# A sketched-attention and expert kernel on one core: GpSimd's last sends behind the branch, VectorE for the last scaling, the head in written order

## The chip, the cores and the metric

The kernel runs on 1 core of one Trainium2 chip. The metric is device microseconds (us) of one execution; the time given is the median of several runs. The engines are called PE (TensorE), DVE (VectorE), ACT (ScalarE), POOL (GpSimd) and SP (SyncE). Each engine has a sequencer that walks through its own instructions in order; the profile writes PEq, DVEq, ACTq, POOLq and SPq for it. A load or store that SP, ACT or POOL issues is carried out by the DMA engines.

## What is computed

An attention block with sketched features, whose output, laid out as 4352 rows of 128, goes through a top-1 mixture of 8 experts with an output gate:

```python
a, b = S1 @ x, S2 @ x                       # phi(x): outer product of two sketches, r = 8, so 64 features
kv = einsum('bhsf,bhsd->bhfd', phi(k), v)
z = sum over s of phi(k)
attn = (phi(q) @ kv) / (phi(q) . z + 1e-6)  # 4 batches, 4 heads, 1088 positions, head size 32
x = attn as 4352 x 128
e = argmax(x @ w_gate); gate = softmax(x @ w_gate)[e]; eom = sigmoid(x @ w_output_gate)
out = gate * eom[e] * (relu(x @ w1[e]) @ w2[e])        # 128 -> 1024 -> 128 in expert e
```

## The kernel before

**Head.** The program begins with small tables. SP loads the two sketch matrices S1 and S2 (line 275, into `bits`, 2 KB each) and after them the first groups of k, q and v (`load`, lines 287 to 293). They are 64-bit numbers; `split` (lines 406 to 427) turns them into two fp32 parts on DVE, `turn_rows` transposes the parts on PE (line 403) and line 436 spreads them over the four heads into `Sb`, the matrix that every sketch multiplies with. While it waits, PE multiplies zeros (`zeros`, line 260). POOL writes the tables that routing needs much later: `ones`, `eio`, `eps`, `ecap`, `carry` (lines 331 to 342) and those of `pool_constants` (line 355); ACT blanks the buffers `kz` and `xin` (line 451) and copies `carry` into the first table of running sums (`choose_carry`, line 688). This part stands outside `tc.manual_schedule()`, so that a scheduler may move its instructions on each engine.

**Body.** Up to line 1124 the order is that of a planner (`Plan`): every step has an engine, a length, a rank (with the table `NUDGE`) and the steps it waits for, and `plan.order()` writes them out, engine by engine in that order. It covers the sketches (`sketch`), products (`both`, `product`), sums over k and v (`sums`), attention (`attend`), the routing of the rows to experts, and the 32 tiles of 128 rows that each expert gets four of whatever the counts are (`NF` = 32). For a tile t: `fetch` (POOL, an indirect DMA of the rows into `xin`), `divide` and `turn_copy` (DVE), `turn` (PE), `up` (PE, 8 products of 128 by 128), `relu` (ACT or DVE in turn), `down` (PE, 8 products), `scale` (ACT, line 929: the gate, from PSUM into `ys`) and `give` (POOL, line 933: an indirect DMA that scatters the rows of `ys` into the output).

**Late tiles.** How many tiles more are needed is known only at run time: a count `nt` (at most 33) is loaded into a register of every engine, and `arm` (line 1089) writes a cascade of nested branches. Arm k runs when nt > k:

```python
with tc.If(now["nt"] > k, label=f"exit{k}") as more:
    expect(k + 1)
    ...                      # loads, up(t), relu(t), down(t - 1)
    scale(t - 1)
    give(t - 1)
    arm(k + 1)
with more.Else():
    down(t - 1); scale(t - 1); give(t - 1)
```

with t = 32 + k. The code of all taken arms follows in one piece, and the Else parts stand behind it, that of the deepest arm first. `expect` puts a hint for the next branch into the programs of PE, ACT and POOL (line 1087: one register instruction and one BRANCH_PREFETCH_HINT). In the runs shown nt is 5: tiles 32 to 36 are late ones, arms 0 to 4 are taken, and at exit5 every engine jumps to an Else part, which holds the end of tile 36.

Of the kernel before, what the change touches and what calls it, by code (L numbers as in the profile page):

```python
# [177 lines left out]
def kernel(  # L178
# [40 lines left out]
    def const(name, shape, dtype=F32):  # L219
        return sbuf.tile(list(shape), dtype, tag=name, name=name)  # L220
# [33 lines left out]

    ys = [const(f"ys{i}", [TS, DM]) for i in range(NY)]
# [13 lines left out]
    for i, x in enumerate((S1, S2)):  # L269
        own = slice(i * r, (i + 1) * r)  # L270
        if wide:
            x, dst, n = x.bitcast(I32), bits[own].rearrange("p d w -> p (d w)"), 2 * D
        else:
            dst, n = plain[own], D
        nc.sync.dma_start(dst, bass.AP(tensor=x.tensor, offset=x.offset, ap=[[n, r], [1, n]]))
# [49 lines left out]
    for h in range(H):  # L325
        nc.vector.memset(maskh[h * D:(h + 1) * D, h:h + 1], 1.0)
    mask0 = const("mask0", [128, 1])
# [4 lines left out]
    nc.gpsimd.memset(ones, 1.0)  # L332
    eio = const("eio", [128, E])
    for e in range(E):
        nc.gpsimd.memset(eio[:, e:e + 1], float(e))
    eps = const("eps", [128, 1])
    nc.gpsimd.memset(eps, EPS)
    ecap = const("ecap", [128, E])
    nc.gpsimd.tensor_scalar_mul(ecap, eio, float(CAP))
    carry = const("carry", [128, E])  # L340
    nc.gpsimd.memset(carry, 0.0)
    nc.gpsimd.tensor_copy(carry[0:1], ecap[0:1])
# [42 lines left out]
    before, efirst, exs = pool_constants()  # L385
# [13 lines left out]
    turned_rows = ps_t()  # L399
    Sb = const("Sb", [128, 2, H, 2 * r])  # L400

    def turn_rows(i):
        nc.tensor.transpose(turned_rows[:, 2 * r * i:2 * r * (i + 1)], rows[i].rearrange("p h d -> p (h d)"), ident[:2 * r, :2 * r])
        zeros(1)

    def split():
# [20 lines left out]
        turn_rows(1)  # L427
    if wide:
        split()
    else:  # L430
        nc.vector.tensor_copy(rows[0], plain.unsqueeze(1).to_broadcast((2 * r, H, D)))
        turn_rows(0)
        nc.vector.memset(rows[1], 0.0)
        turn_rows(1)
    for i in range(2):
        nc.vector.tensor_mul(Sb[:, i], bview(turned_rows[:, 2 * r * i:2 * r * (i + 1)], [[0, H], [1, 2 * r]]),
                             bview(maskh, [[1, H], [0, 2 * r]]))

    selr = const("selr", [2 * D, 2])
    nc.vector.memset(selr, 0.0)  # L440
    for i in range(2):
        nc.vector.memset(selr[D * i:D * (i + 1), i:i + 1], 1.0)
# [555 lines left out]
    for i, rs in enumerate(routes):  # L998
# [6 lines left out]
        add(f"CC{i}", "ACT", 210, k, prior, lambda i=i: choose_carry(i))  # L1005
# [79 lines left out]
    def expect(k):  # L1085
        if k < NL:
            tc.mark_branch_hint_location(f"exit{k}", hint=now["nt"] > k, engines=[mybir.EngineType.PE, mybir.EngineType.Activation, mybir.EngineType.Pool])

    def arm(k):
        t = NF + k  # L1090
        if k == NL:
            down(t - 1)
            scale(t - 1)
            give(t - 1)
            return
        rings = (ps_t, ps_w, ps_y)
        kept = [(list(x.free), dict(x.lent)) for x in rings]
        with tc.If(now["nt"] > k, label=f"exit{k}") as more:
            expect(k + 1)
            if AHEAD <= k + 2 < NL:  # L1100
                fetch_weights(t + 2)
            if LA <= k + 3 < NL:
                fetch(t + 3)
            up(t)
            if LT <= k + 1 < NL:
                divide(t + 1)
                turn(t + 1)
                turn_copy(t + 1)
            relu(t, t % 2 == 0)
            down(t - 1)  # L1110
            scale(t - 1)
            give(t - 1)
            arm(k + 1)
        for x, (free, lent) in zip(rings, kept):
            x.free, x.lent = free, lent
        with more.Else():
            down(t - 1)
            scale(t - 1)
            give(t - 1)

    with tc.manual_schedule():
        for name in plan.order():
            plan.ops[name]["emit"]()
        arm(0)
# [36 lines left out]
```

## Time and profile before

| what | value |
|---|---|
| time, median of 3 runs | 208.14 us (207.84 to 208.62) |
| the profiled execution's own time | 208.37 us |
| its span | 206.6 us |
| PE busy | 193.3 us, 94% of the span |
| DVE, ACT, POOL busy | 105.1, 73.0, 87.4 us |
| loads and stores | 32.02 MB |

The span reaches from the first to the last instruction that the profiler recorded; the time has 1.8 us more around it. Busy time is given by engine; the time of a sequencer's own instructions (waits, branches, semaphores, issuing of DMAs) is not in it. In a timeline row the first number is the start in us from the span's start, the second the duration, and the bracket says how long the engine stood idle before it and what ended that. A row such as "MATMUL y<-xall,hT" names the tile written and the tiles read.

### The profile page before, as it was taken

The numbers are of one execution on the slowest core, as the hardware profiler recorded it, in microseconds if no ns is written. First come the engines' busy times: TensorE is split into PE (matmuls) and PEld (weight loads), VectorE is DVE, ScalarE is ACT, GpSimd is POOL, SyncE is SP. The second block draws the span as 40 slices with busy tenths as digits, with TensorE's granted clock in tenths as the row PEclk, the third lists the DMA queues.
The fourth block names the chain that finished last, engine by engine and source line by source line (L and its number), as shares of the span: only waits on it lengthen the run. The fifth ranks groups of instructions, "written<-read, shape, count | busy, mean of one in ns | idle before, by whom it ended". The sixth has DMA issues, their size and how long they took to land.

```text
span 206.6 us, 6180 instructions
## 1 busy us (share of the span) xinstructions
PE 193.3 (94%) x2530; PEld 185.8 (90%) x2530; DVE 105.1 (51%) x287; ACT 73.0 (35%) x173; POOL 87.4 (42%) x116
## 2 busy tenths in 40 slices
PE   7799999997999999999999989999999999999960
PEld 6699898876799999899999989999999999999960
DVE  5777878898774554775497144204312434311300
ACT  7226575476764244341132121231223022123120
POOL 8100000003826423767365727365347635354631
PEclk9789999999999999999999999999999999999996
DMA  4998878671259991271149992111101101016010
GB/s 143 337 360 241 285 263 286 206 230 41 64 141 344 312 376 32 70 246 57 37 123 405 412 416 83 52 32 48 40 20 50 49 12 53 18 33 219 16 38 13
DMA packets 14934, 32.02 MB, mean 155 GB/s; under 512 B 2489, under 2 KB 7751, under 8 KB 14000
## 3 DMA queue, kind: packets, MB, share of 16 engines
q1 hardware_dynamic: 9488, 17.49, 24.9%
q10 hardware_dynamic: 2304, 8.39, 11.5%
q0 software_dynamic: 3104, 5.65, 9.1%
q8 instruction: 22, 0.36, 0.7%
q14 instruction: 16, 0.13, 0.2%
HBM read 26.47 MB, written 5.84 MB: 156 GB/s over the span
## 4 chain that ended last, share of the span: by engine, by line
PE 51%; issue 17%; DMA 9%; POOL 8%; DVE 7%; ACT 4%; POOLq 1%; SPq 1%
PE w L913 15%; PE acc L926 8%; PE y L926 8%; PE w L496 5%; DMA xin<-xt,putf 5%; PE acc L559 4%; POOL out_dram L933 4%; POOL xin L889 4%; PE w L636 3%; PE w L609 3%; DMA kT<-in_k_dram 2%; DMA out_dram<-ys,putfar 2%; ACT xall L649 2%; ACT qpT L615 1%; PE t L903 1%
## 5 line engine op out<-in xcount | busy, mean ns | idle before, releaser
L889 POOL DMA_INDIRECT xin<-xt,putf x32 | 35.1, 1096 | 80.9 <-DVE ab L525 43.6
L913 PE MATMUL w<-xsT,wt 128*128 128x128 f32 x512 | 61.3, 275 | 0.0
L913 PEld LDWEIGHTS w<-xsT,wt 128*128 128x128 f32 x512 | 59.3, 192 | 0.2
L933 POOL DMA_INDIRECT out_dram<-ys,putf x32 | 34.0, 1064 | 16.1 <-ACT ys L929 8.2
L917 ACT ACTIVATE hT<-w 128x1024 f32<-128x1024 f32 x23 | 23.5, 1024 | 40.7 <-PE w L913 40.7
L926 PE MATMUL acc<-wt,hT 128*128 128x128 f32 x256 | 31.3, 275 | 0.7 <-DVE hT L919 0.7
L926 PE MATMUL y<-wt,hT 128*128 128x128 f32 x256 | 31.4, 276 | 0.0
L926 PEld LDWEIGHTS acc<-wt,hT 128*128 128x128 f32 x256 | 29.9, 192 | 0.9 <-issue 0.9
L919 DVE TENSOR_SCALAR hT<-w 128x1024 f32<-128x1024 f32 x14 | 17.1, 1223 | 25.9 <-PE w L913 24.4
L926 PEld LDWEIGHTS y<-wt,hT 128*128 128x128 f32 x256 | 30.0, 192 | 0.0
L906 DVE COPY xsT<-t 128x128 f32<-128x128 f32 x38 | 10.3, 286 | 24.8 <-PE t L903 24.8
L929 ACT ACTIVATE ys<-y,xin 128x128 f32<-128x128 f32 x19 | 7.0, 367 | 39.7 <-PE y L926 34.8
L899 DVE TENSOR_TENSOR xdiv<-xin 128x128 f32<-128x128 f32 x38 | 10.6, 286 | 20.2 <-DMA xin<-xt,putf 12.4
L929 ACT ACTIVATE ys<-acc,xin 128x128 f32<-128x128 f32 x18 | 6.6, 367 | 19.7 <-PE acc L926 19.0
L889 POOL DMA_INDIRECT xin<-xt,putfar x8 | 8.4, 1047 | 9.9 <-ACT ys L929 7.7
L559 PE MATMUL acc<-vt,kp 128*64 128x65 f32 (+1 forms) x288 | 11.7, 229 | 0.0
L559 PEld LDWEIGHTS acc<-vt,kp 128*64 128x64 f32 (+1 forms) x288 | 9.9, 140 | 1.9 <-issue 0.4
L636 PEld LDWEIGHTS w<-kz,qpT 64*64 64x64 f32 x544 | 8.7, 134 | 2.7 <-ACT qpT L615 1.8
L536 DVE TENSOR_TENSOR kp<-ab 128x1024 f32<-128x1024 f32 (+1 forms) x9 | 10.5, 1163 | 1.1 <-PE acc L559 1.0
L636 PE MATMUL w<-kz,qpT 64*64 64x49 f32 x544 | 9.7, 220 | 1.4 <-ACT qpT L615 1.1
L536 DVE TENSOR_TENSOR qp<-ab 128x1024 f32<-128x1024 f32 (+1 forms) x9 | 10.4, 1161 | 0.9 <-PE w L609 0.8
L520 ACT COPY ab<-w 128x256 f32<-128x256 f32 (+1 forms) x18 | 6.5, 359 | 11.4 <-PE w L496 7.2
(166 smaller groups left out, 222.2 us busy)
## 6 DMA issues: line engine op xcount, KB each, us to landing
wt<-in_w_dram ACTq DMA_DIRECT2D x16, 512.0 KB, 6.5
xall<-in_w_dram SPq DMA_DIRECT2D x3, 1024.0 KB, 7.5
xt<-xall SPq DMA_DIRECT2D x2, 1176.0 KB, 10.6
vt<-in_v_dram SPq DMA_DIRECT2D x8, 260.0 KB, 5.3
kT<-in_k_dram SPq DMA_DIRECT2D x8, 256.0 KB, 3.9
qT<-in_q_dram SPq DMA_DIRECT2D x8, 256.0 KB, 3.8
kp<-in_w_dram SPq DMA_DIRECT2D x2, 1024.0 KB, 16.3
qp<-in_w_dram SPq DMA_DIRECT2D x1, 1024.0 KB, 10.5
```

What stands on the lines that cost most here:

```text
L496: nc.tensor.matmul(ps[:, j].rearrange("p i x -> p (i x)"), src[:, j * 128:(j + 1) * 128], Sb.rearrange("p i h x -> p (i h x)"), start=True ...
L536: (nc.gpsimd if (w, g) in ASIDE else nc.vector).tensor_mul(res[:, :n], bview(av, [list(av.ap[1]), list(av.ap[2]), [0, r]]), bview(bv, [lis ...
L559: nc.tensor.matmul(now["acc", b][64 * h:64 * (h + 1), s], kp[p0:p0 + n, heads_at("k", g, j, s) + h].rearrange("s i j -> s (i j)"), now["v" ...
L636: nc.tensor.matmul(ps[64 * t:64 * (t + 1), h, 2 * j + s], now["qT", g][64 * h:64 * (h + 1), 2 * j + s, 64 * t:64 * (t + 1)], kz[(c * 128 + ...
L889: nc.gpsimd.indirect_dma_start(out=xin[t % NX], out_offset=None, in_=xt[:n, :], in_offset=bass.IndirectOffsetOnAxis(ap=index(t), axis=0), ...
L899: nc.vector.tensor_mul(xdiv[t % 2].rearrange("p (k d) -> p k d", d=D), x[:, :, :D], x[:, :, D].unsqueeze(2).to_broadcast((TS, H, D)))
L913: nc.tensor.matmul(ps[:, c], w[:, c], xsT[t % 4], start=True, stop=True)
L917: nc.scalar.activation(hTs[t % 2], now["h", t], ACTF.Relu)
L919: nc.vector.tensor_scalar_max(hTs[t % 2], now["h", t], 0.0)
L926: nc.tensor.matmul(ps, hTs[t % 2][:, c], w[:, c], start=(c == 0), stop=(c == FC - 1))
L929: nc.scalar.activation(ys[t % NY], now["y", t], ACTF.Copy, scale=xin[t % NX][:, VZ:VZ + 1])
L933: apart("out", nc.gpsimd.indirect_dma_start(out=out, out_offset=bass.IndirectOffsetOnAxis(ap=index(t), axis=0), in_=ys[t % NY], in_offset= ...
```

## The change

- **Last sends.** In arm k (from k = 1) `give(t - 2)` is issued at the start of the arm, and `give(t - 1)` no longer at its end; the Else part, now a function `leave(k)`, issues both `give(t - 2)` and `give(t - 1)`. In POOL's program the branch of exit k+1 thereby stands ahead of the send of tile t - 1.
- **Last scaling.** In the Else part the scaling of the last tile is done by DVE (`scale_last`) and no longer by ACT.
- **Hints.** `expect` gives its hint to PE alone.
- **Head.** `tc.manual_schedule()` is entered at the start, so that the head keeps the order in which it is written. S2 is loaded by ACT's queue. The two transposes get a PSUM tile each, and each has its zeros behind it. `selr` is made early. POOL's tables (now `small_constants` and `pool_constants`) come after a copy that reads `Sb`, so that POOL waits for it. The copy of `carry` on ACT gets an earliest time of 15 us in the planner.

```diff
--- before.py
+++ after.py
@@ -252,6 +252,7 @@
             tc.declare_no_dep(ins.ins, group=g, reason="the rows are distinct")
         tc.add_to_no_dep_group(group, ins.ins)
 
+    ctx.enter_context(tc.manual_schedule())
     ys = [const(f"ys{i}", [TS, DM]) for i in range(NY)]
     idle = ys[0]
     nc.vector.memset(idle, 0.0)
@@ -272,7 +273,7 @@
             x, dst, n = x.bitcast(I32), bits[own].rearrange("p d w -> p (d w)"), 2 * D
         else:
             dst, n = plain[own], D
-        nc.sync.dma_start(dst, bass.AP(tensor=x.tensor, offset=x.offset, ap=[[n, r], [1, n]]))
+        (nc.sync, nc.scalar)[i].dma_start(dst, bass.AP(tensor=x.tensor, offset=x.offset, ap=[[n, r], [1, n]]))
 
     groups = [range(c, min(c + GRP // 128, NC)) for c in range(0, NC, GRP // 128)]
     G = len(groups)
@@ -324,22 +325,28 @@
     nc.vector.memset(maskh, 0.0)
     for h in range(H):
         nc.vector.memset(maskh[h * D:(h + 1) * D, h:h + 1], 1.0)
+    selr = const("selr", [2 * D, 2])
+    nc.vector.memset(selr, 0.0)
+    for i in range(2):
+        nc.vector.memset(selr[D * i:D * (i + 1), i:i + 1], 1.0)
     mask0 = const("mask0", [128, 1])
     nc.vector.memset(mask0, 0.0)
     nc.vector.memset(mask0[0:1], 1.0)
 
     ones = const("ones", [128, 128])
-    nc.gpsimd.memset(ones, 1.0)
     eio = const("eio", [128, E])
-    for e in range(E):
-        nc.gpsimd.memset(eio[:, e:e + 1], float(e))
     eps = const("eps", [128, 1])
-    nc.gpsimd.memset(eps, EPS)
     ecap = const("ecap", [128, E])
-    nc.gpsimd.tensor_scalar_mul(ecap, eio, float(CAP))
     carry = const("carry", [128, E])
-    nc.gpsimd.memset(carry, 0.0)
-    nc.gpsimd.tensor_copy(carry[0:1], ecap[0:1])
+
+    def small_constants():
+        nc.gpsimd.memset(ones, 1.0)
+        for e in range(E):
+            nc.gpsimd.memset(eio[:, e:e + 1], float(e))
+        nc.gpsimd.memset(eps, EPS)
+        nc.gpsimd.tensor_scalar_mul(ecap, eio, float(CAP))
+        nc.gpsimd.memset(carry, 0.0)
+        nc.gpsimd.tensor_copy(carry[0:1], ecap[0:1])
 
     routes, g = [], 0
     for n in ROUTES:
@@ -382,7 +389,6 @@
     names = const("names", [128, NC, 2], B16)
     NX = 6
     xin = [const(f"xin{i}", [TS, W]) for i in range(NX)]
-    before, efirst, exs = pool_constants()
     late = {}
 
     def late_constants():
@@ -396,12 +402,15 @@
             full = late["full", j] = const(f"full{j}", [128, E])
             nc.gpsimd.tensor_scalar(full, ecap, 1.0, float((j + 1) * TS), op0=ALU.mult, op1=ALU.add)
 
-    turned_rows = ps_t()
+    turned_rows = [ps_t() for _ in range(2)]
     Sb = const("Sb", [128, 2, H, 2 * r])
 
     def turn_rows(i):
-        nc.tensor.transpose(turned_rows[:, 2 * r * i:2 * r * (i + 1)], rows[i].rearrange("p h d -> p (h d)"), ident[:2 * r, :2 * r])
+        nc.tensor.transpose(turned_rows[i][:, :2 * r], rows[i].rearrange("p h d -> p (h d)"), ident[:2 * r, :2 * r])
         zeros(1)
+
+    def spread_rows(i):
+        nc.vector.tensor_mul(Sb[:, i], bview(turned_rows[i][:, :2 * r], [[0, H], [1, 2 * r]]), bview(maskh, [[1, H], [0, 2 * r]]))
 
     def split():
         SHL, SHR, OR = ALU.logical_shift_left, ALU.logical_shift_right, ALU.bitwise_or
@@ -425,6 +434,8 @@
         nc.vector.scalar_tensor_tensor(out=scale, in0=scale, scalar=23, in1=sign, op0=SHL, op1=OR)
         nc.vector.tensor_mul(rows[1], heads(plain), heads(scale.bitcast(F32)))
         turn_rows(1)
+        spread_rows(0)
+        spread_rows(1)
     if wide:
         split()
     else:
@@ -432,14 +443,12 @@
         turn_rows(0)
         nc.vector.memset(rows[1], 0.0)
         turn_rows(1)
-    for i in range(2):
-        nc.vector.tensor_mul(Sb[:, i], bview(turned_rows[:, 2 * r * i:2 * r * (i + 1)], [[0, H], [1, 2 * r]]),
-                             bview(maskh, [[1, H], [0, 2 * r]]))
-
-    selr = const("selr", [2 * D, 2])
-    nc.vector.memset(selr, 0.0)
-    for i in range(2):
-        nc.vector.memset(selr[D * i:D * (i + 1), i:i + 1], 1.0)
+        spread_rows(0)
+        spread_rows(1)
+    nc.gpsimd.tensor_copy(ecap[:, :1], Sb[:, 1, 0, :1])
+    small_constants()
+    before, efirst, exs = pool_constants()
+
     wgb = const("wgb", [2 * D, 2, 2, 2 * E])
 
     def gates_spread():
@@ -1002,7 +1011,7 @@
         if i - 1 in MARKS:
             prior = [f"CT{i - 1}"]
         add(f"CA{i}", "DVE", 110 * n + 350, k, [f"X{lastg}"], lambda i=i: choose_first(i))
-        add(f"CC{i}", "ACT", 210, k, prior, lambda i=i: choose_carry(i))
+        add(f"CC{i}", "ACT", 210, k, prior, lambda i=i: choose_carry(i), at=15000)
         add(f"CB{i}", "DVE", 45 * n + 600, k, [f"CA{i}", f"CC{i}"], lambda i=i: choose_second(i))
         add(f"CE{i}", "ACT", 700, k, [f"CB{i}"], lambda i=i: choose_exp(i))
         add(f"PL{i}", "PE", 350, k, [f"CB{i}"], lambda i=i: place(i), take="t", words=16)
@@ -1084,19 +1093,31 @@
 
     def expect(k):
         if k < NL:
-            tc.mark_branch_hint_location(f"exit{k}", hint=now["nt"] > k, engines=[mybir.EngineType.PE, mybir.EngineType.Activation, mybir.EngineType.Pool])
+            tc.mark_branch_hint_location(f"exit{k}", hint=now["nt"] > k, engines=[mybir.EngineType.PE])
+
+    def scale_last(t):
+        nc.vector.tensor_scalar_mul(ys[t % NY], now["y", t], xin[t % NX][:, VZ:VZ + 1])
+        ps_y.back(t)
+
+    def leave(k):
+        t = NF + k
+        if k:
+            give(t - 2)
+        down(t - 1)
+        scale_last(t - 1)
+        give(t - 1)
 
     def arm(k):
         t = NF + k
         if k == NL:
-            down(t - 1)
-            scale(t - 1)
-            give(t - 1)
+            leave(k)
             return
         rings = (ps_t, ps_w, ps_y)
         kept = [(list(x.free), dict(x.lent)) for x in rings]
         with tc.If(now["nt"] > k, label=f"exit{k}") as more:
             expect(k + 1)
+            if k:
+                give(t - 2)
             if AHEAD <= k + 2 < NL:
                 fetch_weights(t + 2)
             if LA <= k + 3 < NL:
@@ -1109,19 +1130,15 @@
             relu(t, t % 2 == 0)
             down(t - 1)
             scale(t - 1)
-            give(t - 1)
             arm(k + 1)
         for x, (free, lent) in zip(rings, kept):
             x.free, x.lent = free, lent
         with more.Else():
-            down(t - 1)
-            scale(t - 1)
-            give(t - 1)
-
-    with tc.manual_schedule():
-        for name in plan.order():
-            plan.ops[name]["emit"]()
-        arm(0)
+            leave(k)
+
+    for name in plan.order():
+        plan.ops[name]["emit"]()
+    arm(0)
 
 
 # ---- launch: one core; the arrays laid out as they lie on chip ----
```

**POOL around the branches.** In POOL's program before, this is arm 4, the last one taken, and the branch of exit5; `xin` numbers end in the tile's buffer (tile 39), `ys_75` is tile 35's result.

```order
L1098 COMPARE_AND_BRANCH
L1087 REGISTER_ALU
L1157 BRANCH_PREFETCH_HINT
L889 DMA xin_155<-xt,putfar 128x196
L933 DMA out_dram<-ys_75,putfar 4352x128
L1098 COMPARE_AND_BRANCH
```

The same place in the changed program (line numbers are those of the new file; `ys_75` is now tile 33's, `ys_76` tile 34's, `xin_148` tile 39's buffer):

```order
L942 DMA out_dram<-ys_75,putfar 4352x128
L898 DMA xin_147<-xt,putfar 128x196
L1117 COMPARE_AND_BRANCH
L942 DMA out_dram<-ys_76,putfar 4352x128
L898 DMA xin_148<-xt,putfar 128x196
L1117 COMPARE_AND_BRANCH
```

The two hint instructions are gone, the send of the tile before comes first in the arm, and the branch follows the fetch, with no send between them; the order of sends and fetches to each other is the same.

**POOL in the Else part of exit5.** Before, with what each row waits for (DMASW: a semaphore of one of POOL's DMAs); `ys_70` is tile 36's result (the last row begins the next Else part):

```order
L1157 ISA [waits DMASW4_49]
L933 DMA out_dram<-ys_70,putfar 4352x128 [waits DMASW4_49,Activation_49]
L1098 ISA [waits DMASW5_49,DMASW3_49,DMASW6_49,DMASW2_49,DMASW7_49,DMASW1_49,DMASW0_49]
L1098 UNCONDITIONAL_BRANCH
L1157 ISA [waits DMASW2_49]
```

In the changed program, where `ys_77` is tile 35's result and `ys_72` tile 36's:

```order
L1174 ISA [waits DMASW3_49]
L942 DMA out_dram<-ys_77,putfar 4352x128 [waits DMASW3_49,Activation_49]
L1174 ISA [waits DMASW4_49]
L942 DMA out_dram<-ys_72,putfar 4352x128 [waits DMASW4_49,DVE_49]
L1117 ISA [waits DMASW5_49,DMASW6_49,DMASW2_49,DMASW7_49,DMASW1_49,DMASW0_49]
L1117 UNCONDITIONAL_BRANCH
```

There are two sends where one was; the first waits for ACT's scaling, the second for DVE's.

**POOL at the head.** Before, behind the start of the program:

```order
masks.py:197 MEMSET ident 128x128
L332 MEMSET ones 128x128
masks.py:199 ISA
masks.py:199 AFFINE_SELECT ident<-ident 128x128
L335 MEMSET eio 128x1 x8
L337 MEMSET eps 128x1
L341 MEMSET carry 128x8
```

In the changed program:

```order
masks.py:197 MEMSET ident 128x128
masks.py:199 ISA
masks.py:199 AFFINE_SELECT ident<-ident 128x128
L448 COPY ecap<-Sb 128x1
L343 MEMSET ones 128x128
L345 MEMSET eio 128x1 x8
L346 MEMSET eps 128x1
L347 TENSOR_SCALAR ecap<-eio 128x8
```

All tables but `ident` now stand behind a copy that reads `Sb`, the last result of the split on DVE.

## Rows read from the trace of the kernel before

**Rows 1.** Busy us by engine, PE's granted clock, DMA share and GB/s, by stretch.

```profile
core 0: us, PE busy (x) PEld busy (x) DVE busy (x) ACT busy (x) POOL busy (x), PEclk, DMA share, GB/s
4.56:7.97 3.41, 1.65 (x67) 1.35 (x68) 1.83 (x5) 1.06 (x4) 1.22 (x7) 1.00 0.94 299
7.97:11.39 3.42, 3.42 (x52) 3.08 (x54) 2.49 (x5) 0.74 (x2) 0.00 (x0) 0.50 1.03 375
11.39:199.60 188.21, 184.76 (x2404) 178.20 (x2401) 98.41 (x256) 67.06 (x156) 81.47 (x76) 1.00 0.46 154
```

**Rows 2.** Timeline of the end, from 196 us: start, duration, engine, line, operation.

```profile
197.63 1.95 PE L926 MATMUL y<-xall,hT 128*128 128x128 f32 x16
197.84 0.37 ACT L929 ACTIVATE ys<-acc,xin 128x128 f32<-128x128 f32 x1 [0.81 <-PE acc L926]
198.48 1.00 POOL L933 DMA_INDIRECT out_dram<-ys,putfar  x1 [1.34 <-ACT ys L929]
200.61 0.37 ACT L929 ACTIVATE ys<-y,xin 128x128 f32<-128x128 f32 x1 [2.41 <-issue]
202.30 0.98 POOL L933 DMA_INDIRECT out_dram<-ys,putfar  x1 [2.83 <-DMA out_dram<-ys,putfar]
```

**Rows 3.** Sequencer instructions, 195 to 202 us: ns min/median/max, first and last start.

```profile
L1098 POOLq COMPARE_BRANCH  x1: 78/78/78, 198.2 to 198.2; - x1
L933 POOLq MOVE  x1: 38/38/38, 201.1 to 201.1; - x1
L1098 DVEq COMPARE_BRANCH  x1: 67/67/67, 196.1 to 196.1; - x1
L1098 DVEq EVENT_SEMAPHORE  x1: 21/21/21, 196.6 to 196.6; - x1
```

**Rows 4.** Chain of waits, 193 to 197.2 us: start, us, what.

```profile
194.56 0.03 POOLq L1098
...
194.76 0.03 POOLq L889
...
195.38 0.03 POOLq L933
...
196.10 1.04 POOL xin L889
```

**Rows 5.** Instructions of the program's end, from 203 us, as in rows 3.

```profile
L1157 SPq EVENT_SEMAPHORE  x14: 17/28/28, 204.9 to 206.5; - x14
```

**Rows 6.** The page's costliest groups: a DVE operation on 128 by 128 from PSUM.

```profile
L906 DVE COPY xsT<-t 128x128 f32<-128x128 f32 x38 | 10.3, 286 | 24.8 <-PE t L903 24.8
```

**Rows 7.** Chain of waits, 0 to 8 us.

```profile
1.28 0.29 SPq L275
...
1.62 0.36 SPq L293
...
2.97 4.74 DMA kT<-in_k_dram
```

**Rows 8.** Timeline of PE, 4.4 to 10 us.

```profile
7.85 1.94 PE L496 MATMUL w<-Sb,kT 128*128 128x128 f32 x8 [1.13 <-DMA kT<-in_k_dram]
```

**Rows 9.** Timeline of DVE, 0 to 14 us.

```profile
2.71 0.21 DVE L413 TENSOR_SCALAR bit<-bits 16x32 int32<-16x32 int32 x1 [1.01 <-DMA bits<-in_S_dram]
...
3.25 0.49 DVE L417 TENSOR_SCALAR bit<-bit 16x32 int32<-16x32 int32 x1
...
5.15 0.35 DVE L436 TENSOR_TENSOR Sb<-t,maskh 128x64 f32<-128x64 f32 x2 [0.33 <-PE t L403]
...
7.18 1.23 DVE L536 TENSOR_TENSOR kp<-ab 128x1024 f32<-128x1024 f32 x1
...
10.23 0.42 DVE L525 TENSOR_TENSOR ab<-w,ab 128x256 f32<-128x256 f32 x1 [0.23 <-ACT ab L520]
...
11.32 0.42 DVE L525 TENSOR_TENSOR ab<-w,ab 128x256 f32<-128x256 f32 x1 [0.67 <-ACT ab L520]
```

**Rows 10.** Timeline of POOL, 0 to 7 us: first and last table.

```profile
0.96 0.20 POOL L332 MEMSET ones<- 128x128 f32 x1
...
5.51 0.35 POOL L397 TENSOR_SCALAR full<-ecap 128x8 f32<-128x8 f32 x2
```

## The prediction, made before the changed kernel ran

> **What bounds the kernel now.** Look first at busy time by stretch [rows 1]: from 11.39 to 199.6 us PE works 184.8 of 188.2 us, so no other engine matters there unless it makes PE wait. What is left is the two ends: the head, until PE has data, and the 7 us between PE's last product and the end of the span.
>
> The end is read from the timeline [rows 2]. PE begins the last tile's products (tile 36, Else part of exit5) at 197.63 and ends them at 199.58. ACT ended tile 35's scaling at 198.21 and starts tile 36's only at 200.61; for those 2.41 us the row names "issue", that is, ACT waited for nothing the profile shows, and for 1.0 us of them PE had been done. POOL sends tile 35 at 198.48 and tile 36 at 202.30. That row puts the wait down to the landing of a store, but the sequencer's own rows tell otherwise [rows 3]: POOL branches at 198.2 and executes the first instruction of the Else part at 201.1. These 2.9 us are the jump; from there to the send's start are another 1.2 (201.1 to 202.30). ACT's gap is the same kind of jump. DVE jumped at 196.1 and went on at 196.6. So the end of the kernel is: scaling of tile 35, POOL's send, POOL's jump, the last send. Behind it comes a fixed tail of 4.3 us (202.30 to the span's 206.6): the store lands and SP runs its last waits from 204.9 [rows 5].
>
> The head's chain [rows 7] runs over SP's queue: S1, S2 (from 1.28), the first k group from 1.62, and the k group that PE waits for, issued at 2.97 and under way for 4.74 us. PE starts on it at 7.85 after 1.13 us idle, and works without a gap from there [rows 1, 8].
>
> **The end, step by step.** Before, the sequencer comes to the branch of exit5 only when the send of tile 35 has its data (198.2, right behind ACT's end at 198.21), because that send stands ahead of it. In the changed order only the fetch of tile 39 does. When does POOL get there? In arm 4 the row behind that fetch, the MOVE of the next send, runs at 195.38, before the fetch itself starts (196.10) [rows 4]: the sequencer runs ahead. The branch takes this place. The branch, test and hint that stood between tile 34's send and the fetch (194.56 to 194.76) no longer do, so I put it at 195.2. Plus 2.9 of jump: 198.1; plus 1.2 to the send: tile 35 starts at 199.3 (before: 198.48, so this one is later, and nobody waits for it). A send takes 1.00 and the next one starts about 0.3 behind it, as the gaps between POOL's DMAs show (its row of 195.38 led to a start at 196.10, 0.3 behind the 1.00 of the send before): tile 36 starts at 200.6 if its data is there.
>
> It is there: DVE ends its own jump early even if it now costs 2.9 us (196.1 + 2.9 = 199.0, still ahead of PE's 199.58). Its code grows by one scaling in each Else part, so I do not assume that it keeps the 0.5 us of before. The scaling on DVE is bounded below by a copy of 128 by 128 from PSUM, 286 ns [rows 6], and above by ACT's 0.37 [rows 2]; I take 0.3, the same shape on the same engine: done at 199.9. A send starts 0.27 behind its scaling (198.21 to 198.48), so DVE's bound is 200.2 and POOL's 200.6 decides. **The term: 202.30 - 200.6 = 1.7 us gained.** Its ends: 2.1, if the jump were hidden wholly; 0, if the last send stays behind something else.
>
> Queued behind each moved send is only the fetch that also followed it before, as the order shows; sends and fetches keep their sequence, so no fetch comes later and PE's arms do not change. ACT's and POOL's hint instructions cost about 0.1 us an arm on sequencers that wait for PE and ACT anyway: nothing. Without a hint those engines might stop at a taken arm; DVE has none before and PE has no gap that would show it. ACT's Else part shrinks to a jump that must end before the last waits; it has from 198 to 203.
>
> **The head, step by step.** With S2 on ACT's queue SP issues the first k group at 1.28 instead of 1.62, and everything behind it 0.34 us earlier. The awaited k group should land 0.34 earlier and PE start at 7.5. **The term: 0.3 us**, between 0 (the memory system sets the landing, with DMA busy at 0.94 of its time in 4.56 to 7.97 [rows 1]) and 0.7, if also the half-clock stretch below shrinks. It counts only if the sketch matrix `Sb` is ready: before at 5.5 (5.15 + 0.35 [rows 9]), followed by two sketches that PE finishes at 6.7, so it has 1.13 us to spare. The split starts when the matrices land (2.71), about 0.4 earlier with two queues; written order puts dependent steps next to each other, which may cost some tenths; I take that pair as nothing. The two zeros moved behind the transposes lie in the same idle time. ACT's table load and blanking come one DMA issue later (SP's second one took 0.29 [rows 7]); the same 1.13 us cover that. The copy of `carry`, `selr`, the second PSUM tile: nothing, hidden by the same wait.
>
> POOL's tables move from 0.96 to 5.86 [rows 10] to about 5.5 to 10.4, under DVE's first products. Their readers come with the routing, far later. What they can cost is DVE's speed. Below, the split of before shows it: in its 2.8 us under the same POOL work one operation took 0.49 instead of some 0.2 [rows 9], 0.3 lost; for 4.9 us of tables that is 0.5. Above, DVE stands still for all 4.9. DVE waits 0.23 and 0.67 us before the additions at 10.23 and 11.32, so 0.9 is free; I take the lower price, which is the same pair of engines, and it is hidden.
>
> [...]
>
> **The sum.** The profiled execution took 208.37: minus 1.7, minus 0.3, is 206.4. The median of the runs lies 0.23 lower, at 208.14, so the forecast is **206.1 us**, 1.0% less. A measurement of this kernel can tell about 0.5% (1.0 us) from no change.
>
> **Rivals.**
> - *The jump is paid again.* Two sends make the Else part longer, and POOL might stop a second time between them. The last send would then start at 199.3 + 2.9 + 1.2 = 203.4, 1.1 later than before; with the head 208.9. For it: POOL had one such stop. Against: behind its first instruction the old Else part ran through. The same class holds the case that POOL does not reach the branch early: 207.8. Chance 0.13. [...]
> - *POOL's tables slow DVE's first products.* Place: 5.5 to 10.4 us. If DVE lost all 4.9 us, 4.0 would reach PE: 206.1 + 4.0 = 210.1, slower than before. It decides from a loss of 0.9 + 2.0 = 2.9 us on, ten times what the one stretched operation shows. Against it: that row. Chance 0.07 of losing over 1 us, half of it on the slower side.
> - *PE's clock in the head.* [...] Chance 0.06 and 0.05.
>
> **How the numbers follow.** The forecast's own case, with the head between 0 and 0.7 and the end between 1.3 and 2.1, gives 205.3 to 206.8, with a chance of 0.69. The range of 205.2 to 207.6 adds the tables' case up to 1.5 us and leaves out the second jump and the clock's cases, 0.2 in all. Faster by over 0.5% (below 207.1) are the forecast, the missing half-clock stretch and part of the tables' case: 0.77. Within 0.5%: one more half-clock stretch and most of the jumps: 0.17. Slower: 0.06, tables and a second jump on top of a failed head.
>
> **What would show it.** Right: POOL's branch of exit5 near 195.2 on the old scale, tile 35's send about 1 us later than before, the last send 1.3 behind it, DVE's scaling right behind PE's end, ACT with no operation behind 198.6; SP's first k load at 1.28 and PE's wait for the k group ending near 7.5. Wrong: a gap of 2 us or more between the last two sends, a DVE scaling over 0.3 us behind PE's end, or products near 7 us of much over 1.23.

## The result and the profile after

| | before | after |
|---|---|---|
| median of 4 runs | 208.38 us (207.84 to 208.62) | 205.75 us (205.44 to 206.69) |
| the profiled execution's own time | 208.37 us | 205.64 us |
| its span | 206.6 us | 203.8 us |

The ratio is 0.9885, 95% interval 0.9846 to 0.9924: 2.4 us less. The forecast was 206.1 us. The ratios of this document leave out runs that took over 1.5% longer than the fastest of the same kernel.

The timeline of the changed kernel's end, as [rows 2] showed it before:

```profile
196.26 1.95 PE L935 MATMUL y<-xall,hT 128*128 128x128 f32 x16
196.47 0.37 ACT L938 ACTIVATE ys<-acc,xin 128x128 f32<-128x128 f32 x1 [0.81 <-PE acc L935]
197.76 1.00 POOL L942 DMA_INDIRECT out_dram<-ys,putfar  x1 [1.98 <-DMA out_dram<-ys,putf]
198.43 0.35 DVE L1099 TENSOR_SCALAR ys<-y,xin 128x128 f32<-128x128 f32 x1 [3.46 <-PE y L935]
199.06 0.98 POOL L942 DMA_INDIRECT out_dram<-ys,putfar  x1 [0.30 <-DVE ys L1099]
```

PE ends at 198.21 (196.26 + 1.95), DVE scales 0.22 behind it, the last send starts 0.85 behind PE's end. Before it was 2.72 (202.30 - 199.58). So the last send came **1.87 us closer to PE's end**. The sequencers' own instructions say how (L1117 is the branch, L942 the send; ns min/median/max, first and last start):

```profile
L1117 POOLq COMPARE_BRANCH  x1: 53/53/53, 193.8 to 193.8; - x1
...
L942 POOLq MOVE  x2: 29/34/38, 196.6 to 197.5; - x2
...
L1117 ACTq COMPARE_BRANCH  x1: 50/50/50, 196.5 to 196.5; - x1
```

POOL branches at 193.8, 4.4 us ahead of PE's end and ahead of tile 35's data, and executes the first instruction of the Else part at 196.6. The jump of some 2.8 us is still there, as in [rows 3], but now lies under PE's last products. ACT leaves at 196.5 with nothing more to scale.

Behind the last send the two profiles differ too. This is its row with the landing, from the view of line L933 before and of L942 after:

```profile
L933 POOL DMA_INDIRECT out_dram<-ys,putfar x1: 977/977/977, 202.3 to 202.3; - x1
...
DMA to landing us min/median/max: 2.6/2.6/2.6
```

```profile
L942 POOL DMA_INDIRECT out_dram<-ys,putfar x1: 977/977/977, 199.1 to 199.1; - x1
...
DMA to landing us min/median/max: 3.1/3.1/3.1
```

The last store now needs 3.1 us to land, not 2.6, so that the span ends 4.74 us behind the last send (203.8 - 199.06), not 4.3. Thus 0.44 of the 1.87 is given back in this pair of executions; how far that holds for others is taken up below. The spans differ by 2.8 us: 1.87 - 0.44 at the end, and 1.37 because PE itself ends earlier (198.21, before 199.58). Of that third part 0.82 comes from the head. SP's first k load and PE's timeline from 3.9 us:

```profile
1.28 0.83 SPq L294 DMA_DIRECT2D kT<-in_k_dram  x2
```

```profile
3.90 0.80 PE L263 MATMUL w<-ys 128*128 128x128 f32 x2
4.63 0.28 PE L409 MATMUL t<-ident,rows 16*128 16x16 f32 x1
4.84 0.80 PE L263 MATMUL w<-ys 128*128 128x128 f32 x2
5.57 1.99 PE L494 MATMUL w<-Sb,kT 64*64 64x64 f32 x64
7.65 2.01 PE L505 MATMUL w<-Sb,kT 128*128 128x128 f32 x8
```

PE has no idle time in front of the sketch at 7.65, where it waited 1.13 us for a k group [rows 8]. But the work ahead of it is slow: the first sketch takes 1.99 us. The same 64 products took 1.16 in an execution at full clock (after_again, below), and the 8 products of the sketch at 7.65 take 2.01, where before they took 1.94 [rows 8] at a granted clock of 0.50 [rows 1]. So PE ran at about half clock here (an estimate from these durations: the profile has no record of the granted clock in this stretch). The chain of waits of the head, from 4.9 us, names what the sketch at 7.65 waits for:

```profile
4.91 0.72 PE w L263 x2
5.64 1.11 PE w L494 x32
...
6.77 0.38 ACT ab L529
...
7.17 0.44 DVE ab L534
...
7.65 2.01 PE w L505 x8
```

Zeros, first sketch, its copy out of PSUM by ACT and an addition on DVE: no load of k stands in it any more (ahead of these pieces the chain leads over the transposes and the split to the load of the sketch matrices). In this execution the granted clock rose to 1.00 at 9.47 us, against 11.39 before [rows 1], and from 12 us on PE ran 0.82 us ahead of the old kernel. The other 0.55 of the 1.37 arises between 47 and 122 us, where executions differ by as much without a cause that was found (the send_old of below loses 1.2 us there).

### The profile page after: what moved, and what is told of

Its sections match the earlier page's. It is cut to its first block, busy times and chain, and to the rows that moved or that the text cites. A ratio compares the mean times of both kernels' runs of the same rounds, so it can differ in the third digit from the quotient of the medians.

```text
span 203.8 us, 6158 instructions
## 1 busy us (share of the span) xinstructions
PE 193.8 (95%) x2530; PEld 186.3 (91%) x2530; DVE 105.2 (52%) x288; ACT 73.0 (36%) x172; POOL 89.7 (44%) x117
## 4 chain that ended last, share of the span: by engine, by line
PE 53%; issue 16%; DMA 8%; DVE 8%; POOL 8%; ACT 4%; POOLq 1%; DVEq 0%
PE w L922 17%; PE acc L935 9%; PE y L935 9%; POOL out_dram L942 5%; PE w L505 4%; DMA xin<-xt,putfar 4%; DMA xin<-xt,putf 4%; PE w L645 3%; POOL xin L898 3%; PE acc L568 3%; PE w L618 3%; PE t L912 2%; ACT qpT L624 1%; ACT xall L658 1%; PE w L494 1%
## 5 line engine op out<-in xcount | busy, mean ns | idle before, releaser
L898 POOL DMA_INDIRECT xin<-xt,putf x32 | 34.2, 1069 | 72.7 <-DVE qp L545 34.5
L942 POOL DMA_INDIRECT out_dram<-ys,putf x32 | 33.4, 1043 | 16.3 <-ACT ys L938 8.3
L618 PE MATMUL w<-ident,qp 128*128 128x128 f32 x68 | 9.3, 279 | 0.9 <-issue 0.4
```

The source lines that it names most:

```text
L618: nc.tensor.transpose(ps[:, 2 * j + s], qp[:, heads_at("q", g, j, s):heads_at("q", g, j, s) + 2].rearrange("p h i j -> p (h i j)"), ident)
L898: nc.gpsimd.indirect_dma_start(out=xin[t % NX], out_offset=None, in_=xt[:n, :], in_offset=bass.IndirectOffsetOnAxis(ap=index(t), axis=0), ...
L942: apart("out", nc.gpsimd.indirect_dma_start(out=out, out_offset=bass.IndirectOffsetOnAxis(ap=index(t), axis=0), in_=ys[t % NY], in_offset= ...
```

## The experiments

Each kernel is compared with the kernel before, run on the same chip. In the first group before took 208.85 us (median), in the second 208.55.

**Which half brings how much.** tail_only is the kernel before with the edits of the end alone (hints, `leave`, `scale_last`, the place of `give`); head_only has those of the head alone. The core of tail_only's diff against before:

```diff
-            tc.mark_branch_hint_location(f"exit{k}", hint=now["nt"] > k, engines=[mybir.EngineType.PE, mybir.EngineType.Activation, mybir.EngineType.Pool])
+            tc.mark_branch_hint_location(f"exit{k}", hint=now["nt"] > k, engines=[mybir.EngineType.PE])
...
+            if k:
+                give(t - 2)
...
-            give(t - 1)
...
-            down(t - 1)
-            scale(t - 1)
-            give(t - 1)
+            leave(k)
```

And of head_only's:

```diff
+    ctx.enter_context(tc.manual_schedule())
...
-        nc.sync.dma_start(dst, bass.AP(tensor=x.tensor, offset=x.offset, ap=[[n, r], [1, n]]))
+        (nc.sync, nc.scalar)[i].dma_start(dst, bass.AP(tensor=x.tensor, offset=x.offset, ap=[[n, r], [1, n]]))
...
+    nc.gpsimd.tensor_copy(ecap[:, :1], Sb[:, 1, 0, :1])
+    small_constants()
+    before, efirst, exs = pool_constants()
```

> The kernel before with the change's end alone (sends behind the branch, VectorE's last scaling, hints for TensorE alone); head as before. Theory A (the end is worth what the two traces show between PE's end and the span's end: 206.6 - 199.58 = 7.0 before, 203.8 - 198.21 = 5.6 after): 1.4 us faster than before, last send 0.85 us behind PE's end. Rival B (most of the gain is the head's): under 0.7 us faster.

> The kernel before with the change's head alone; the end with its sends, scaling and hints as before. Theory A: 0.3 to 1.4 us faster (0.3 from the earlier loads, the rest by where the half-clock stretch lies in the head and so by execution). Rival B: 1.4 us or more. Rival C (the 1.37 us by which PE ended earlier in the changed kernel's profile are chance): within 0.3 us of before.

tail_only: ratio 0.9942 (0.9907 to 0.9978), 1.2 us less. head_only: 0.9952 (0.9916 to 0.9988), 1.0 us less. Together 2.2, which lies within the interval of the whole gain (1.6 to 3.2). The timelines of both ends, tail_only first:

```profile
198.04 1.95 PE L926 MATMUL y<-xall,hT 128*128 128x128 f32 x16
...
199.52 1.00 POOL L933 DMA_INDIRECT out_dram<-ys,putfar  x1 [1.97 <-DMA out_dram<-ys,putf]
200.21 0.35 DVE L1090 TENSOR_SCALAR ys<-y,xin 128x128 f32<-128x128 f32 x1 [3.46 <-PE y L926]
200.84 0.98 POOL L933 DMA_INDIRECT out_dram<-ys,putfar  x1 [0.32 <-DVE ys L1090]
```

```profile
197.78 1.95 PE L935 MATMUL y<-xall,hT 128*128 128x128 f32 x16
...
200.73 0.37 ACT L938 ACTIVATE ys<-y,xin 128x128 f32<-128x128 f32 x1 [2.39 <-PE y L935]
202.31 0.99 POOL L942 DMA_INDIRECT out_dram<-ys,putfar  x1 [2.70 <-DMA xin<-xt,putfar]
```

With the end's edits alone the last send is 0.85 us behind PE's end, as in the changed kernel; without them 2.58, as before. The landing took 3.1 us in tail_only too, so its net gain at the end, 1.4, lies within its measured interval (0.5 to 1.9 us). Nothing here shows that one half depends on the other, but each is known only to some 0.7 us. For head_only the interval is 0.3 to 1.8 us: it bears out a gain, and theory A's range, but does not exclude rival B, and rival C lies at its edge. Its own profiled execution, with 208.00 us close to the median, does not show the gain: PE ends at 199.73, 0.15 later than before.

**Which edit of the end.** act_scales is the changed kernel with `scale(t - 1)` by ACT in place of `scale_last`; send_old has DVE's scaling, but POOL's sends in their old places. act_scales, in `leave`:

```diff
-        scale_last(t - 1)
+        scale(t - 1)
```

send_old, in `leave` and `arm`:

```diff
-        if k:
-            give(t - 2)
...
-            if k:
-                give(t - 2)
...
             scale(t - 1)
+            give(t - 1)
             arm(k + 1)
```

> The changed kernel, with the last tile's scaling given back to ScalarE. Theory A (ScalarE's own jump takes 2.6 us from the end of tile 35's scaling, so it can scale only 1.0 us behind PE's end): 0.7 to 0.9 us slower than the changed kernel, last send near 1.9 us behind PE's end. Rival (the scaling was hidden behind GpSimd's jump): same as the changed kernel.

> The changed kernel, with GpSimd's send of tile t-1 at the end of the arm again, ahead of the branch; VectorE keeps the last scaling. Theory A (the jump of 2.8 us begins only when tile 35 is scaled): 1.5 to 1.9 us slower than the changed kernel, last send 2.7 us behind PE's end as before. Rival (the ScalarE jump was the limit, and VectorE alone mends it): under 0.5 us slower.

The timelines of the ends, act_scales first:

```profile
196.64 1.95 PE L935 MATMUL y<-xall,hT 128*128 128x128 f32 x16
...
199.60 0.37 ACT L938 ACTIVATE ys<-y,xin 128x128 f32<-128x128 f32 x1 [2.40 <-issue]
200.25 0.98 POOL L942 DMA_INDIRECT out_dram<-ys,putfar  x1 [1.35 <-ACT ys L938]
```

```profile
197.66 1.95 PE L935 MATMUL y<-xall,hT 128*128 128x128 f32 x16
...
199.83 0.35 DVE L1099 TENSOR_SCALAR ys<-y,xin 128x128 f32<-128x128 f32 x1 [3.46 <-DMA xin<-xt,putfar]
202.21 0.98 POOL L942 DMA_INDIRECT out_dram<-ys,putfar  x1 [2.71 <-DMA xin<-xt,putfar]
```

With ACT's scaling the last send is 1.66 us behind PE's end, 0.81 worse, and POOL waits for ACT, whose jump of 2.4 us stands in front of its scaling. With the old sends it is 2.60 behind, 1.75 worse, although DVE has scaled in time. So it takes both edits for the whole gain of 1.87 in the place of the last send: the moved sends alone gain 1.06 (2.72 - 1.66) and then stop at ACT's jump, the moved scaling alone gains 0.12 (2.72 - 2.60). The ratios are 0.9965 (0.9917 to 1.0013) and 0.9946 (0.9901 to 0.9991), which fits but separates neither from the changed kernel; the profile's rows decide here.

**The head and the clock.** The second group began with the changed kernel again.

> The changed kernel itself, as the yardstick of its group. Both theories: about 2.6 us below the kernel before (ratio 0.984 to 0.992), last send 0.8 to 0.9 us behind PE's end. How far PE is ahead of the kernel before by 12 us should follow from when its granted clock rises to 1.00: ahead by 0.8 if at 9.5, by 0.2 if at 10.7.

after_again: 0.9925 (0.9885 to 0.9965), 1.6 us less, a little short of what was expected. Its profiled execution, 204.92 us, is the fastest of any, and PE's timeline in its head explains it:

```profile
5.35 1.16 PE L494 MATMUL w<-Sb,kT 64*64 64x64 f32 x64
7.10 1.13 PE L505 MATMUL w<-Sb,kT 128*128 128x128 f32 x8 [0.58 <-DMA kT<-in_k_dram]
8.59 0.69 PE L494 MATMUL w<-Sb,qT 64*64 64x64 f32 x32 [0.36 <-DVE ab L534]
```

The granted clock was full from 4.80 us and did not fall while PE worked. Now PE waits for the k group again and starts on it at 7.10, 0.75 us earlier than in [rows 8]. This table puts the profiled executions together: when the granted clock rose for the last time in the head, when the sketch of the third k group began, and how far ahead of the kernel before PE was at the product that before starts at 12.1 us (PE's products of two traces put side by side in their order).

| kernel | clock full from | sketch at | PE ahead by |
|---|---|---|---|
| before (old head) | 11.39 (and 4.56 to 7.97) | 7.85 | 0 |
| tail_only (old head) | 10.69 | 8.15 | 0.03 |
| head_only | 10.72 | 7.75 | 0.24 |
| after_third | 10.18 | 7.64 | 0.54 |
| hints_back | 9.73 | 7.57 | 0.78 |
| after | 9.47 | 7.65 | 0.82 |
| act_scales | 8.83 | 7.66 | 1.12 |
| send_old | 8.56 | 7.67 | 1.15 |
| after_again | 4.80 | 7.10 | 1.82 |
| sp_loads_both | 11.70 | 7.95 | -0.27 |
| no_gate | 9.45 | 7.95 | 0.67 |
| zeros_first | 10.22 | 7.26 | 0.75 |
| zeros_first_2 | 10.96 (and 4.13 to 7.54) | 7.45 | 0.39 |
| zeros_more | 9.46 | 9.05 | 0.17 |

With the same head, PE's lead follows the moment of the rise. The old and the new head with the same rise (tail_only, head_only) differ by 0.2 us. The seven executions with the whole new head average a lead of 0.92 us; the two of the old head average 0.02. That is about the 1.0 us of head_only's time, but it links the two only on average, since the lead does not stay: behind 47 us it changes by up to 1.2 us. At PE's end it is 1.74 in after_again, 1.37 in after, 0.99 in act_scales, -0.03 in send_old and -0.15 in head_only, and -0.42 in tail_only with the old head. Why it changes there was not found. Whether the new head makes the clock rise earlier, or two executions of the old one were not its usual ones, is open: no more than two of it were profiled.

**Single edits of the head.** sp_loads_both has S2 on SP's queue again; zeros_first has seven products of zeros at the start and none behind the transposes; zeros_more puts four products of zeros behind the second sketch, under the wait for the third k group, and moves one from behind the first transpose to the start. In this order:

```diff
-        (nc.sync, nc.scalar)[i].dma_start(dst, bass.AP(tensor=x.tensor, offset=x.offset, ap=[[n, r], [1, n]]))
+        nc.sync.dma_start(dst, bass.AP(tensor=x.tensor, offset=x.offset, ap=[[n, r], [1, n]]))
```

```diff
-WARM = 5
+WARM = 7
...
-        zeros(1)
```

```diff
-WARM = 5
+WARM = 6
...
-        zeros(1)
+        if i:
+            zeros(1)
...
+        if (w, g) == ("k", 1):
+            for _ in range(4):
+                nc.tensor.matmul(turned_rows[0][:, 128:256], idle, idle, start=True, stop=True)
```

> The changed kernel, with both sketch matrices loaded by SP again. Theory A (the first k load at 1.28 instead of 1.62 us is what the head gains): the first k load at 1.6 again, PE's wait for the third k group ends 0.2 to 0.35 later, and the time is 0.2 to 0.4 us above the changed kernel if the granted clock rises at the same moment. Theory B (the gain in the head comes from the granted clock and the order of the split): PE's shift by 12 us follows the clock's rise alone, and the time is within 0.2 us of the changed kernel.

> The changed kernel, with the two products of zeros that stand behind the transposes moved ahead of both (seven in a row at the start). Theory A (the zeros behind the second transpose hold the first sketch back, to 5.57 us): the first sketch starts at 5.0 to 5.2, when the sketch matrix is ready, and PE has 0.4 us more slack ahead of the third k group, which sets the pace anyway; the time stays within 0.5 us of the changed kernel unless the granted clock rises at another moment. Theory B (PE's activity ahead of 5 us sets when the granted clock rises): with zeros in one stretch the clock is full from about 5 us, as in the kernel before, but falls again while PE waits for the third k group; the sketches of 7.6 to 11 us run at half clock and the time is that of the changed kernel or up to 1 us longer.

> The changed kernel, with one product of zeros moved from behind the first transpose to the start, and four more of them behind the second sketch, where PE otherwise waits for the third k group (from 7.56 us on in the changed kernel, earlier at full clock). Theory B (the half clock of the head comes from PE's idle stretch ahead of the third k group): the granted clock rises before 9.46, the sketches of 7.6 to 9.7 take 1.0 to 1.2 us each pair instead of 2.0, PE is 0.5 to 1.0 us further ahead by 12 us and the time is 0.3 to 1.0 us below the changed kernel. Theory A (k groups set the pace and zeros only delay them): no earlier, up to 0.5 us longer.

sp_loads_both: 0.9924 (0.9887 to 0.9962), the same as after_again. In its profile SP's first k load is at 1.62 again, and the whole chain of the head stands 0.3 later (first sketch 5.86, the third k group's 7.95). So theory A's mechanism shows in the rows. The time cannot tell 0.3 us from nothing (the interval is 0.8 us wide to each side), and at 12 us little of it is left: the table's trend, carried on from after and head_only to a rise at 11.70, gives a lead of -0.2 (an estimate), and the execution has -0.27.

zeros_first: 0.9871 (0.9817 to 0.9926), from 6 runs. The first sketch starts right behind the spread of its matrix, as theory A says (PE's timeline):

```profile
5.15 1.99 PE L493 MATMUL w<-Sb,kT 64*64 64x64 f32 x64 [0.34 <-DVE Sb L412]
7.26 2.05 PE L504 MATMUL w<-Sb,kT 128*128 128x128 f32 x8
```

The third k group's sketch follows 0.4 earlier than in the profile of after. It is 0.75 ahead at a rise of 10.22, where after_third has 0.54 at 10.18: about 0.2 us better at the same clock. By the ratios it is 1.1 us below after_again, more than theory A's 0.5, but the two intervals overlap.

zeros_more: 0.9992 (0.9957 to 1.0027), the whole gain gone (PE's timeline):

```profile
5.26 1.99 PE L495 MATMUL w<-Sb,kT 64*64 64x64 f32 x64
7.18 2.07 PE L510 MATMUL t<-ys 128*128 128x128 f32 x8
9.05 1.26 PE L506 MATMUL w<-Sb,kT 128*128 128x128 f32 x8
```

The zeros took 2.07 us, where 8 products of the same shape take 1.16 at full clock (the sketch that starts at 11.30 us in the profile of after), so they ran at about half clock, and the k group's sketch came at 9.05, 1.4 us late. The clock rose at 9.46, as in after (9.47). Theory B's zeros did not bring the clock back sooner in this execution; that they only delay is what the rows and the time show.

**Hints, tables, and zeros again.** The third group ran on another chip, where the granted clock fell to half once more in the body (54.1 to 64.3 us in hints_back). The kernel before took 222.76 us there, with a mean granted clock of 0.96 to 0.98 by run, so the times of this group are compared only with each other. hints_back gives the hints to ACT and POOL again, no_gate puts POOL's tables back to the start without the copy of `Sb`; zeros_first_2 and after_third are zeros_first and the changed kernel once more.

hints_back, in `expect`, and no_gate:

```diff
-            tc.mark_branch_hint_location(f"exit{k}", hint=now["nt"] > k, engines=[mybir.EngineType.PE])
+            tc.mark_branch_hint_location(f"exit{k}", hint=now["nt"] > k, engines=[mybir.EngineType.PE, mybir.EngineType.Activation, mybir.EngineType.Pool])
```

```diff
+    small_constants()
+    before, efirst, exs = pool_constants()
...
-    nc.gpsimd.tensor_copy(ecap[:, :1], Sb[:, 1, 0, :1])
-    small_constants()
-    before, efirst, exs = pool_constants()
```

> The changed kernel, with the branch hints in the programs of ACT and POOL again. Theory A (hints cost these two about 0.1 us an arm in sequencers that wait anyway, and do not spare them the jump at exit5): the last send stays 0.8 to 1.0 us behind PE's end, POOL takes 2.7 to 2.9 us from its branch of exit5 to the next instruction, and the time is within 0.4 us of the changed kernel. Theory B (the hints hold the branch back where it decides): POOL's branch 0.2 to 0.4 us later against PE's end, the last send 1.1 to 1.3 us behind PE's end, and the time that much longer.

> The changed kernel, with POOL's tables at the start again, not behind a copy that reads the sketch matrix. Theory A (the tables cost little in either place): DVE's products near 7 us stay at 1.23, POOL's tables take 0.2 to 0.4 us each in place of up to 1.3, the sketch matrix is ready at most 0.3 us later, and the time is within 0.4 us of the changed kernel. Theory B (the tables under the split hold the sketch matrix back by over 0.5 us): the first sketch starts at 6.1 or later and the third k group's sketch follows it, 0.3 us or more behind that of the changed kernel.

> Again the changed kernel with all seven products of zeros ahead of the transposes, beside the changed kernel on the same chip. Theory A (the sketch then starts when its matrix is ready, 0.2 to 0.4 us earlier, and the third k group's sketch with it): 0.2 to 0.5 us below the changed kernel. Theory B (the moment at which the granted clock rises differs by execution and outweighs this): the medians differ by no more than the spread of the runs, and the sketch of the third k group starts where its data lands, as in the changed kernel.

> The changed kernel itself, as the yardstick of its group. Both theories: 1.6 to 2.6 us below the kernel before, as in the two groups before; last send 0.8 to 0.9 us behind PE's end; PE's lead by 12 us follows the moment at which its granted clock rises, 0.8 us at 9.5 and 1.8 at 4.8.

Medians: hints_back 220.42 us (ratio 0.9920, 0.9877 to 0.9963), no_gate 220.81 (0.9925, 0.9884 to 0.9966), after_third 220.57 (no ratio: a single run is left for it), zeros_first_2 219.20 (its ratio, 0.9756, rests on two of its 6 runs and is not used). Of hints_back the sequencer's rows (L1117 the branch, L942 the send) and two rows of its end:

```profile
L1117 POOLq COMPARE_BRANCH  x1: 78/78/78, 207.9 to 207.9; - x1
...
L942 POOLq MOVE  x2: 29/34/38, 210.5 to 211.5; - x2
```

```profile
210.31 1.95 PE L935 MATMUL y<-xall,hT 128*128 128x128 f32 x16
...
213.10 0.99 POOL L942 DMA_INDIRECT out_dram<-ys,putfar  x1 [0.41 <-DVE ys L1099]
```

POOL branches 4.4 us ahead of PE's end (212.26), as in the changed kernel, jumps for some 2.6, and the last send is 0.84 behind PE's end. So the hints neither hold POOL back nor spare it the jump: theory A. Two more executions bear this out: the kernel before and head_only have the hints as well, and their POOL jumped for 2.9 [rows 3] and 2.7 us. no_gate starts the first sketch at 5.87, 0.3 later than after, with the third k group's sketch at 7.95; theory B's limit of 6.1 is not reached, though its 0.3 us for the third k group's sketch just is. At the same rise of the clock (9.45) the gate, the copy of `Sb` that POOL's tables wait for, is worth 0.15 us at 12 us.

The median of zeros_first_2 is 1.4 us below that of after_third, but this decides nothing: in its profile the half-clock stretch in the body lasted 6.8 us where after_third had 10.2. Its head also shows theory B's case: a clock that is full from 4.13, and falls at 7.54 after PE had waited 1.31 us for the k group. Placing all zeros first is the one version seen that may beat the changed kernel; by these runs it isn't settled.

## Why the prediction came out right

**The end: right in its mechanism, 0.3 us too high in its size.** On the old scale (1.37 us added) POOL's branch stood at 195.2, as the step put it; the jump took 2.8 for 2.9; tile 35's send started at 199.1 for 199.3, tile 36's at 200.4 for 200.6. DVE's scaling took 0.35 for 0.3 and ended 0.28 ahead of the send: DVE's bound and POOL's came out equal, not 0.4 apart as worked out, so less jump would have gained nothing more in this execution. The step that failed in size is the fixed tail of 4.3 us: the landing of the last store took 3.1 us and not 2.6, with the send before it only 1.30 us ahead instead of 3.8. Why it lands later is not shown, and it does not always do so: from the last send to the end of the span the ten profiled executions with moved sends and DVE's scaling take 3.9 to 4.9 us (mean 4.55), the three with the old sends 3.9 to 4.3 (mean 4.0), and the shortest of the ten, hints_back, has its last two sends just as close, 1.40 us apart. From PE's end to the span's end the means are 5.4 and 6.6. So the end is worth 1.4 us in the first pair of profiles, 1.2 by these means and 1.2 in tail_only's time, where the sum had 1.7.

**The head: right in sign, too small, and the reason given explains only a small part.** The sum took 0.3 us, from SP's first k load. That load did move from 1.62 to 1.28, and the heads compared at the same clock differ by 0.2. The split began 0.24 us earlier, at 2.47, not 0.4. But the time gained is about 1.0 (head_only, 0.3 to 1.8), and the lead in seven profiled executions averages 0.92, beyond the 0.7 that the step allowed. The step that failed is that PE's wait for the k group decides: in most profiled executions PE runs at about half clock there (the first sketch takes 1.99 us, not 1.16) and is not waiting, and the chain of split, transposes, zeros and first sketch sets the pace. What moves PE's lead at 12 us is when the clock rises; why that moment differs from execution to execution stays open. The rival on PE's clock came nearest to this, with a chance of 0.06 for one half-clock stretch more and of 0.05 for none; the runs show instead a lead anywhere from 0.24 to 1.82 us with one and the same head. The upper end is an execution of 204.92 us with the clock full from 4.80; the forecast less a stretch like that of [rows 1], 3.42 us at 0.50 and so 1.7 us, would be 204.4 (an estimate).

The two errors have opposite signs, 0.3 to 0.5 us too much at the end and 0.7 too little in the head. That the forecast's 206.1 stands closer to the result than its terms do is therefore luck in part; the changed kernel measured a second time gained 1.6 us, not 2.4.

**The terms set to nothing.** Hints: nothing, as hints_back shows. POOL's tables under DVE's products: nothing for DVE, but not for the reason given (below). The two zeros behind the transposes do cost: they hold the first sketch to 5.57 us, where zeros_first has 5.15; the cover named for them, the wait for the k group, is gone where the first sketch runs at half clock.

**The rivals.** The jump was not paid again: the sends are 1.30 us apart. The tables did not slow DVE: its products stayed at 1.23, and the up to 1.5 us that the range held for them no run shows.

## What to carry to other kernels

In these profiles the jump to the last Else part took POOL and ACT 2.4 to 2.9 us each, wherever it fell; issue work that waits for late data behind the branch, and the jump goes under the wait, as POOL's 2.8 us did under PE's last products. Moving it on one engine gains only as far as the jump of the next engine on the same chain: here 1.06 us of 1.87. Ahead of a change in the head, look at the clock of that stretch first, since a wait for data seen at full clock, here the 1.13 us of [rows 8], may not be there at half: the profile after had none.

## What the runs showed of the hardware that was not expected

POOL's tables met DVE's products, and it was POOL's instructions that took longer. The timelines of POOL and then DVE in the changed kernel:

```profile
8.31 0.69 POOL L377 CAST sidx<-counts 128x128 bf16<-128x128 int32 x1
8.96 0.21 POOL L379 IOTA tiles<- 128x32 int32 x1
9.23 1.28 POOL L380 CAST cfix<-tiles 128x32 f32<-128x32 int32 x1
...
11.51 1.23 POOL L400 TENSOR_SCALAR stepT<-step 128x33 f32<-128x33 f32 x1
```

```profile
7.63 1.23 DVE L545 TENSOR_TENSOR kp<-ab 128x1024 f32<-128x1024 f32 x1
...
9.22 1.23 DVE L545 TENSOR_TENSOR kp<-ab 128x1024 f32<-128x1024 f32 x1
...
11.42 1.23 DVE L545 TENSOR_TENSOR kp<-ab 128x1024 f32<-128x1024 f32 x1 [0.23 <-PE acc L568]
```

The cast at 9.23 began 0.01 us behind a product and ended 0.06 behind it, at 10.51; in no_gate, ahead of any product, POOL's timeline has for the same instructions:

```profile
4.31 0.29 POOL L377 CAST sidx<-counts 128x128 bf16<-128x128 int32 x1
...
4.83 0.21 POOL L380 CAST cfix<-tiles 128x32 f32<-128x32 int32 x1
...
6.04 0.23 POOL L402 TENSOR_SCALAR stepT<-step 128x33 f32<-128x33 f32 x1
```

So 0.21 became 1.28, and 0.23 became 1.23 (`stepT`), while an iota, whose row names no tile read, kept its time under a product (the one at 8.01 took 0.24 us, in no_gate 0.24) and DVE's products their 1.23. Both times DVE's product had begun first, 0.01 us ahead of the cast at 9.23 and 0.09 ahead of `stepT`, and POOL's instruction ended right behind it: at 10.51, the product at 10.45; at 12.74, the product at 12.65. The opposite order, POOL first, no row here shows. The prediction had weighed the overlap as a loss for DVE; here it was POOL's, and POOL had time.

The second surprise is the spread of the clock's rise, 4.80 to 10.72 us in executions of one and the same head. It is of the size of the whole effect of the head, and a single profile of either kernel would not have shown it.
